# A fused attention and two-MLP kernel: q, k and v laid out by the host, and the scale moved into the step that takes the minimum

## The chip, the cores and the metric

The kernel runs on one core of one Trainium2 chip, as a single launch. The metric is the device time of an execution in microseconds; the work that the host does on the arrays before the launch is not in it.

## What is computed

The reference has three stages. The first is causal attention over a batch of 4, 8 heads, 576 tokens and a head size of 64, with a bias from a running sum:

```python
scores = scale * np.matmul(q, k.transpose(0, 1, 3, 2))
cum = np.cumsum(np.maximum(s, 0.0), axis=-1)
bias = -(cum[:, :, :, None] - cum[:, :, None, :])
scores = np.where(causal, -1000000000.0, scores + np.minimum(bias, 0.0))
...
attn = np.exp(scores)
attn = attn / (np.sum(attn, axis=-1, keepdims=True) + 1e-09)
return np.matmul(attn, v).astype(np.float32)
```

Its result is laid out as 2304 tokens by 512. The second stage is an MLP of 512 to 2048 to 512, `(s * relu(x @ w_in)**2 + b) @ w_out`. The third takes the elementwise maximum of three products, `max(x @ w1, x @ w2, x @ w3) @ w_out`, 512 to 768 to 512. Everything is float32.

## The kernel before, in words

**Stages.** The MLPs run as products of values split into two parts (`mm3`, lines 242 to 246: three matmuls for each product). The hidden units of the first MLP are halved: the first half ("a") is computed while attention still runs, the second half ("b") after it, and then comes the third stage. The weights are split into their two parts on the fly (`weight_steps`, lines 258 to 289): one load, an ACT step at line 273, and steps on DVE, ACT or POOL.

**Jobs.** Attention works on pairs of heads: 16 pairs, four for each batch. The four pairs of the first batch are done in two jobs each, "A" (queries 0 to 319) and "B" (the others); the twelve other pairs are one job "W" each. So there are 20 jobs. For each job the kernel loads q and k with tokens on the partitions (`load_tokens`, lines 427 to 434: one DMA for each head's full chunks of 128 tokens at line 432, and one for a remainder at line 434), turns chunks of both heads on TensorE (`turn`, line 476), and copies them out of PSUM on ACT or DVE (`copy_qk`, line 486, through `copy`, lines 233 to 237); the copy of q multiplies by minus the scale. v is loaded by the same `load_tokens` and is used as it lands. The tiles of q and k in turned form, and those of v, alternate between two buffers; the tiles as loaded, `qn` and `kn`, exist once.

**Scores.** A job has up to six units (a chunk of queries by a range of keys). `qk` (lines 488 to 497) writes the scores of both heads of a unit into two PSUM banks (line 493) and adds the bias through a one-hot matrix and the table `dd` (line 495). `least` (line 507, on DVE) adds the causal mask `late_keys`, multiplies by a scale operand that is 1.0, and writes the result and its row minimum. `expo` (line 513, ACT) takes the exponential, `turn_p` (line 554) turns the probabilities on TensorE, `copy_p` takes them out of PSUM, and `av` (line 573) multiplies by v. `x_copy` (line 578) divides by the row sums, and `x_lo` stores x (line 590).

**The start.** s is loaded four times into groups of 32 partitions on ACT's DMA queue (line 327). DVE clears the unused rows of `qn` and `kn` (line 333), clips s (line 339), takes the running sum (line 340) and the differences to the middle of each query chunk (line 345); ACT and DVE split them into `dd` (lines 348 and 349). Meanwhile TensorE runs `warm` (line 449): 26 transposes whose result nobody reads.

**The order.** All steps after the start are put into a list with costs, due times and needs, and a planner (`Plan.order`, lines 89 to 184) lays them out for each engine; each engine then executes its own list in order. Attention steps have due times from a nominal period for a job; MLP steps fill what is left. Three things in that list belong to the change: the needs of the loads (lines 669 to 676), the steps `turn` and `copy` with their share of the ring of four PSUM banks called `sm`, and the assumed lengths of the start on DVE and ACT (line 642). All loads and stores except those of s are issued by SP.

Of the kernel before, what the change touches and what calls it, by code (L numbers as in the profile page):

```python
# [8 lines left out]
F32 = mybir.dt.float32  # L9
# [5 lines left out]
ALU = mybir.AluOpType  # L15
# [3 lines left out]
P = 128  # L19
BIG = 1.0e9  # L20
# [6 lines left out]
WARM = 26  # L27
# [4 lines left out]
Q_LOAD = -15.0  # L32
K_LOAD = -14.0
V_LOAD = 2.0
# [158 lines left out]
def fused_kernel(ctx, tc, q, k, v, s, w_in, w_out, ms, mb, w1, w2, w3, w_fin, out,  # L193
                 f_split=8):
    nc = tc.nc
    B, H, S, D = q.shape
    NT, DM = out.shape
    DFF = w_in.shape[1]
    DF2 = w1.shape[1]
    NP = H // 2  # L200
# [3 lines left out]
    NC = (S + P - 1) // P  # L204
    LAST = S - (NC - 1) * P
# [120 lines left out]
    for g in range(4):  # L326
        nc.scalar.dma_start(s0[g * NH:(g + 1) * NH], s.rearrange("b h s -> (b h) s"))
    qn, kn = (atp.tile([P, NC, 2, D], F32, name=x) for x in ("qn", "kn"))
    vn = [atp.tile([P, NC, 2, D], F32, name=f"vn{i}") for i in range(2)]
    SHORT = (SPLIT // P, NC - 1)  # L330
    for t in (qn, kn):
        for c in SHORT:
            nc.vector.memset(t[LAST:, c], 0.0)
# [9 lines left out]
    def difference(i):  # L343
        mid = QS[i] + QN[i] // 2
        nc.vector.tensor_scalar(df[:, OFF[i]:OFF[i] + W[i]], cum[:, :W[i]], -1.0, cum[:, mid:mid + 1], op0=ALU.mult, op1=ALU.add)
# [20 lines left out]
    nc.gpsimd.affine_select(out=late_keys[:, ZK - P:], in_=late_keys[:, ZK - P:], pattern=[[-1, P]], compare_op=ALU.is_ge, fill=BIG, base=0, channel_multiplier=1)  # L366
# [60 lines left out]
    def load_tokens(dst, src, p, a, b):  # L427

        bt, hp = divmod(p, NP)
        full, rem = divmod(b - a, P)  # L430
        for j in range(2):
            nc.sync.dma_start(dst[:, :full, j, :], src[bt, 2 * hp + j, a:a + full * P, :].rearrange("(c p) d -> p c d", p=P))
        if rem:
            nc.sync.dma_start(dst[:rem, full, :, :], src[bt, 2 * hp:2 * hp + 2, b - rem:b, :].rearrange("h p d -> p h d"))

    def load_q(job):
        load_tokens(qn, q, job.p, job.q0, job.q1)

    def load_k(job):
        load_tokens(kn, k, job.p, 0, job.keys)  # L440

    def load_v(job):
        load_tokens(vn[job.n % 2], v, job.p, 0, job.keys)
# [26 lines left out]
    def turn(job, key, t, a, b):  # L470

        chunks = range((b - a + P - 1) // P)
        for c0 in range(0, len(chunks), 4):
            ps = bank("pr")
            for c in chunks[c0:c0 + 4]:
                nc.tensor.transpose(ps[:, (c - c0) * P:(c - c0 + 1) * P], t[:, c, :, :], ident)  # L476
            end = min(a + (c0 + 4) * P, b)
            pr[key, job.n, c0 // 4] = (ps, slice(a + c0 * P, end), slice(0, end - a - c0 * P))

    def copy_qk(job, key, z, on):  # L480

        to = {"q": qt, "k": kt}[key]
        if job.n not in to:
            to[job.n] = atp.tile([P, S], F32, name=key, tag=f"{key}{job.n % 2}")
        ps, at, fr = pr.pop((key, job.n, z))
        copy(to[job.n][:, at], ps[:, fr], on, -scale if key == "q" else None)

# [11 lines left out]
    def least(job, u, j):  # L499

        i, k0, k1 = UNITS[u][:3]
        n = QN[i]
        if u == job.units[0]:
            mns[job.n, j] = atp.tile([P, NC], F32, name="mn", tag=f"mn{j}{job.n % 2}")
        mn = mns[job.n, j][:n, i:i + 1]
        a = 0 if k1 < W[i] else ZK - max(k1 - k0, P)
        nc.vector.tensor_tensor_reduce(out=pp[j][i][:n, k0:k1], in0=late_keys[:n, a:a + k1 - k0], in1=ps_.pop((job.n, u, j))[:n, :k1 - k0], scale=1.0,  # L507
                                       scalar=mn if k0 else HUGE, op0=ALU.add, op1=ALU.min, accum_out=mn)
# [85 lines left out]
    def bank(name):  # L594
        ring, z = plan.slot(*BANK)
        return psum.tile([P, 512], F32, name=name, tag=f"b{BANK[ring] + z}")
# [45 lines left out]
    for e, cost in (("DVE", 9.75), ("ACT", 8.8), ("Pool", 5.0)):  # L642
        add(("pre", e), e, cost, -1e9, [], lambda: None)
# [8 lines left out]
    for job in jobs:  # L652
# [16 lines left out]
        for key, load, when, src, q0, q1 in (("q", load_q, Q_LOAD, qn, job.q0, job.q1), ("k", load_k, K_LOAD, kn, 0, job.keys)):  # L669
            add((key, n), "SP", (3, q1 - q0), t0 + when, [("turn", key, n - 1)], load, job, **a)  # L670
            z = range(((q1 - q0 + P - 1) // P + 3) // 4)
            add(("turn", key, n), "PE", 0.109 * ((q1 - q0 + P - 1) // P), tp, [(key, n)], turn, job, key, src, q0, q1, take=[("sm", [("copy", key, n, y)]) for y in z], **a)
            for y in z:
                m = min(4 * P, q1 - q0 - y * 4 * P)
                add(("copy", key, n, y), {"ACT": act_ps(m), "DVE": dve_ps(m)}, 0, tp + 0.1, [("turn", key, n)] + [("qk", n - 2, u) for u in range(6)], copy_qk, job, key, y, **a)
        add(("v", n), "SP", (3, job.keys), t0 + V_LOAD, [("av", n - 2, g) for g in (jobs[n - 2].groups if n > 1 else ())], load_v, job, **a)
        add(("oh", n), "Pool", 0.3, tp, [("qk", n - 2, u) for u in range(6)], one_hot, job, **a)

        for x, u in enumerate(units):
# [3 lines left out]
            ready = [("oh", n)] + [("copy", z, n, y) for z in "qk" for y in range(2)]  # L683
# [431 lines left out]

# [23 lines left out]
```

## Time and profile before

| what | before |
|---|---|
| median of 3 runs | 980.51 us (976.75 to 981.84) |
| the profiled execution | 975.74 us |
| its span, first to last instruction | 973.9 us |
| mean granted clock of TensorE | 0.993 of full speed |
| TensorE busy | 98% of the span |
| DVE, ACT, POOL busy | 51%, 47%, 17% |

Times are microseconds from the start of the span unless ns is said. PE is TensorE, PEld its weight loads, which overlap with matmuls; DVE, ACT and POOL are the vector, scalar and general engines; SPq and ACTq are instructions of the queues of SP and ACT, DMA issues among them. Ends of matmuls are modelled, so two neighbours overlap in a list in order of time, and it is the distance of their starts that tells how long each held the engine. "<-" behind an idle time names what ended it.

### The profile page before, as it was taken

To read this page: it belongs to the slowest core of one execution; us is meant where nothing else is said; L and a number is where in the kernel's file an instruction comes from. 1 tells how busy PE (TensorE), PEld (TensorE's weight loads), DVE (VectorE), ACT (ScalarE), POOL (GpSimd) and SP (SyncE) were. 2 spreads that over 40 slices of the span, in tenths; PEclk is the share of its full clock that TensorE was granted. 3 is DMA by queue.
4 is the path that set the end of the run, shared out by engine and by line. 5 is a ranking of instruction groups with operands and counts; after the bars stand their busy time and mean duration, and the time that the engine had idled before them with its cause. 6 is when DMAs were issued, how large, how long until landed. Compare 5 with 4: busy or idle time off the path is not lost.

```text
span 973.9 us, 17863 instructions
## 1 busy us (share of the span) xinstructions
PE 952.4 (98%) x6558; PEld 867.9 (89%) x6558; DVE 495.7 (51%) x1324; ACT 454.3 (47%) x1221; POOL 168.7 (17%) x270
## 2 busy tenths in 40 slices
PE   7899999999999999999999999999999999999997
PEld 5577788888789789999999999999999999999997
DVE  6898867778663432132778786426621222222221
ACT  5888678778774572232555454333321212121111
POOL 2333123212203022222333232220000000000000
PEclk7999999999999999999999999999999999999999
DMA  6655555565442101561444444225220201010000
GB/s 187 175 144 132 149 160 138 167 178 146 137 123 73 52 8 47 190 225 36 128 139 131 132 126 132 81 69 166 62 66 1 63 3 49 17 39 11 2 31 34
DMA packets 120632, 96.11 MB, mean 99 GB/s; under 512 B 70240, under 2 KB 104032, under 8 KB 120544
## 3 DMA queue, kind: packets, MB, share of 16 engines
q1 hardware_dynamic: 120352, 94.67, 32.8%
q8 instruction: 52, 0.85, 0.4%
q10 hardware_dynamic: 192, 0.30, 0.1%
q14 instruction: 36, 0.29, 0.1%
HBM read 67.67 MB, written 27.26 MB: 97 GB/s over the span
## 4 chain that ended last, share of the span: by engine, by line
PE 88%; DMA 4%; DVE 2%; ACT 2%; SPq 1%; issue 1%; POOL 1%; DVEq 0%; ACTq 0%; POOLq 0%
PE mm L244 23%; PE mm L246 22%; PE mm L245 22%; PE ps L493 6%; PE pt L554 6%; PE px L573 5%; PE pr L476 2%; PE ps L495 1%; PE pr L544 1%; DMA wb_in<-wb_d 1%; DMA xs<-x_d 1%; DMA wg<-in_moe_w_in_dram 1%; DMA stage<-in_moe_w_out_dram 0%; POOL ga L240 0%; DMA wst<-in_moe_w_out_dram 0%
## 5 line engine op out<-in xcount | busy, mean ns | idle before, releaser
L244 PE MATMUL mm<-yh,wt 128*128 128x384 f32 x432 | 146.2, 339 | 0.0
L246 PE MATMUL mm<-yh,wt 128*128 128x384 f32 x432 | 146.2, 338 | 0.0
L245 PE MATMUL mm<-yl,wt 128*128 128x384 f32 x432 | 146.2, 338 | 0.0
L1056 DVE TENSOR_TENSOR u<-mm,u 128x384 f32<-128x384 f32 x72 | 40.1, 558 | 190.2 <-PE mm L246 190.2
L909 ACT ACTIVATE g<-g 128x256 f32<-128x256 f32 (+1 forms) x128 | 56.3, 440 | 136.5 <-DVE g L905 135.8
L905 DVE TENSOR_SCALAR g<-mm 128x256 f32<-128x256 f32 (+1 forms) x128 | 58.1, 455 | 78.8 <-PE mm L246 68.1
L513 ACT ACTIVATE pp<-pp,mn 64x64 f32<-64x64 f32 (+4 forms) x160 | 88.4, 556 | 19.1 <-DVE mn L507 18.9
L244 PE MATMUL mm<-xhi,wa_in 128*128 128x320 f32 (+1 forms) x256 | 82.4, 322 | 0.0
L244 PEld LDWEIGHTS mm<-yh,wt 128*128 128x128 f32 x432 | 81.1, 188 | 1.3
L245 PEld LDWEIGHTS mm<-yl,wt 128*128 128x128 f32 x432 | 81.1, 188 | 1.3
L244 PE MATMUL mm<-ga,wa_out 128*128 128x320 f32 (+2 forms) x256 | 82.2, 321 | 0.0
L554 PE MATMUL pt<-ident,pp 128*128 128x128 f32 x480 | 78.0, 281 | 3.2 <-DVE mn L507 1.4
L233 ACT ACTIVATE pt<-pt 128x256 f32<-128x256 f32 (+3 forms) x186 | 74.0, 434 | 15.4 <-PE pt L554 12.1
L240 POOL TENSOR_TENSOR gbl<-g,gbh 128x320 fp32r<-128x320 f32 (+1 forms) x64 | 55.8, 874 | 145.9 <-ACT gbh L233 143.6
L246 PEld LDWEIGHTS mm<-yh,wt 128*128 128x128 f32 x432 | 81.1, 188 | 0.0
L1060 ACT ACTIVATE hh<-u 128x384 fp32r<-128x384 f32 x36 | 18.9, 525 | 133.1 <-DVE u L1056 133.1
L507 DVE CUSTOM_DVE_ANT_0 pp<-late_keys,ps 64x64 f32<-64x64 f32 (+4 forms) x160 | 62.2, 421 | 33.2 <-PE ps L495 32.7
L246 PE MATMUL mm<-ga,wa_out 128*128 128x320 f32 (+2 forms) x256 | 76.0, 297 | 1.8 <-DVE wa_out L288 1.8
L240 POOL TENSOR_TENSOR ga<-g,ga 128x320 fp32r<-128x320 f32 (+1 forms) x64 | 53.3, 833 | 135.3 <-ACT ga L233 119.9
L245 PE MATMUL mm<-xlo,wa_in 128*128 128x320 f32 (+1 forms) x256 | 75.8, 296 | 1.0 <-POOL xlo L240 1.0
L245 PE MATMUL mm<-ga,wa_out 128*128 128x320 f32 (+2 forms) x256 | 75.9, 296 | 0.8 <-POOL ga L240 0.8
L246 PE MATMUL mm<-xbh,wb_in 128*128 128x320 f32 (+1 forms) x256 | 75.8, 296 | 0.0
(172 smaller groups left out, 2364.0 us busy)
## 6 DMA issues: line engine op xcount, KB each, us to landing
wst<-in_moe_w_dram SPq DMA_DIRECT2D x24, 384.0 KB, 3.8
wb_d<-wbs SPq DMA_DIRECT2D x21, 256.0 KB, 2.8
out_dram<-o SPq DMA_DIRECT2D x18, 256.0 KB, 2.0
kn<-in_k_dram SPq DMA_DIRECT2D x32, 128.0 KB, 2.9
vn<-in_v_dram SPq DMA_DIRECT2D x32, 128.0 KB, 2.7
wst<-in_moe_w_out_dram SPq DMA_DIRECT2D x8, 512.0 KB, 4.1
wb_in<-wb_d SPq DMA_DIRECT2D x8, 512.0 KB, 7.2
wb_out<-wb_d SPq DMA_DIRECT2D x8, 512.0 KB, 10.0
```

Source lines behind the costliest of these rows:

```text
L233: nc.scalar.activation(dst, src, AF.Copy, scale=1.0 if scale is None else scale)
L240: ENGINES[on].tensor_tensor(dst, a, b, op=ALU.subtract)
L244: nc.tensor.matmul(ps, lhs[0], rhs[0], start=first, stop=False)
L245: nc.tensor.matmul(ps, lhs[0], rhs[1], start=False, stop=False)
L246: nc.tensor.matmul(ps, lhs[1], rhs[0], start=False, stop=last)
L493: nc.tensor.matmul(ps[:, :k1 - k0], qt[job.n][r, QS[i]:QS[i] + P], kt[job.n][r, k0:k1], start=True, stop=False)
L507: nc.vector.tensor_tensor_reduce(out=pp[j][i][:n, k0:k1], in0=late_keys[:n, a:a + k1 - k0], in1=ps_.pop((job.n, u, j))[:n, :k1 - k0], scal ...
L513: nc.scalar.activation(p[:n, :w], p[:n, :w], AF.Exp, bias=mns[job.n, j][:n, i:i + 1], scale=-1.0, accum_out=sums[job.n % 2][:n, j, i:i + 1])
L554: nc.tensor.transpose(pt[:, c - c0, :], pp[j][i][:, c * P:(c + 1) * P], ident)
L573: nc.tensor.matmul(px_[job.n][hf][j * D:(j + 1) * D, a0 - h0:h1 - h0], vn[job.n % 2][:, c, j, :], columns(job, pr["p", job.n, j], c, c + 1 ...
L905: nc.vector.tensor_scalar(st["g", f], st["u", f][:, :n], 0.0, None, op0=ALU.max)
L909: nc.scalar.activation(st["g", f], st["g", f], AF.Square)
```

## The change

The host lays out q and k as [pair, 2 x 64, tokens] and v as [pair, tokens, 2 x 64]; `kernel()` passes each input through `_lay_out` before the launch. q and k are loaded straight into the two alternating tiles that the score matmuls read, by one DMA each (`load_qk`), and v by one DMA for the full chunks and one for a remainder (`load_v`). `turn` and `copy_qk` are gone, with the tiles `qn` and `kn` and their clearing. A load of q or k now waits for the score matmuls of the job before the last, which read the same tile; before, it waited for the transposes of the last job. The scale goes into `least` as minus the scale; the mask and the bias differences are divided by it beforehand. Two of the four loads of s go to SP's queue. `warm` has 40 transposes instead of 26, and the lengths that the planner assumes for the start are shorter.

```diff
@@ -24,7 +24,7 @@
 ST2 = 3
 COLD = 8
 D_AT = -2.0
-WARM = 26
+WARM = 40
 
 PACE_3 = 2
 
@@ -193,8 +193,9 @@
 def fused_kernel(ctx, tc, q, k, v, s, w_in, w_out, ms, mb, w1, w2, w3, w_fin, out,
                  f_split=8):
     nc = tc.nc
-    B, H, S, D = q.shape
+    B, H, S = s.shape
     NT, DM = out.shape
+    D = DM // H
     DFF = w_in.shape[1]
     DF2 = w1.shape[1]
     NP = H // 2
@@ -324,13 +325,9 @@
     s4 = atp.tile([P, 4, S], F32, name="s4", tag="p3")
     s0, cum, ones, dh = (s4[:, i, :] for i in range(4))
     for g in range(4):
-        nc.scalar.dma_start(s0[g * NH:(g + 1) * NH], s.rearrange("b h s -> (b h) s"))
-    qn, kn = (atp.tile([P, NC, 2, D], F32, name=x) for x in ("qn", "kn"))
+        (nc.sync if g < 2 else nc.scalar).dma_start(s0[g * NH:(g + 1) * NH], s.rearrange("b h s -> (b h) s"))
     vn = [atp.tile([P, NC, 2, D], F32, name=f"vn{i}") for i in range(2)]
     SHORT = (SPLIT // P, NC - 1)
-    for t in (qn, kn):
-        for c in SHORT:
-            nc.vector.memset(t[LAST:, c], 0.0)
     nc.vector.memset(ones, 1.0)
     lower = const.tile([P, 1], F32, name="lower")
     nc.vector.memset(lower, 0.0)
@@ -342,7 +339,7 @@
     df = atp.tile([P, OFF[-1] + W[-1]], F32, name="df", tag="p2")
     def difference(i):
         mid = QS[i] + QN[i] // 2
-        nc.vector.tensor_scalar(df[:, OFF[i]:OFF[i] + W[i]], cum[:, :W[i]], -1.0, cum[:, mid:mid + 1], op0=ALU.mult, op1=ALU.add)
+        nc.vector.tensor_scalar(df[:, OFF[i]:OFF[i] + W[i]], cum[:, :W[i]], cum[:, mid:mid + 1], 1.0 / scale, op0=ALU.subtract, op1=ALU.mult)
 
     def split_d(a, b):
         nc.scalar.activation(dh[:, :b - a].bitcast(F32R), df[:, a:b], AF.Copy)
@@ -363,7 +360,7 @@
     ZK = W[NC - 2]
     late_keys = atp.tile([P, ZK], F32, name="late_keys")
     nc.gpsimd.memset(late_keys, 0.0)
-    nc.gpsimd.affine_select(out=late_keys[:, ZK - P:], in_=late_keys[:, ZK - P:], pattern=[[-1, P]], compare_op=ALU.is_ge, fill=BIG, base=0, channel_multiplier=1)
+    nc.gpsimd.affine_select(out=late_keys[:, ZK - P:], in_=late_keys[:, ZK - P:], pattern=[[-1, P]], compare_op=ALU.is_ge, fill=-BIG / scale, base=0, channel_multiplier=1)
 
     for t in vn:
         for c in SHORT:
@@ -424,23 +421,19 @@
         nc.sync.dma_start(s_sb, ms.partition_broadcast(P))
         nc.sync.dma_start(b_sb, mb.partition_broadcast(P))
 
-    def load_tokens(dst, src, p, a, b):
-
-        bt, hp = divmod(p, NP)
-        full, rem = divmod(b - a, P)
-        for j in range(2):
-            nc.sync.dma_start(dst[:, :full, j, :], src[bt, 2 * hp + j, a:a + full * P, :].rearrange("(c p) d -> p c d", p=P))
+    def load_qk(job, key):
+
+        to, src, a, b = (qt, q, job.q0, job.q1) if key == "q" else (kt, k, 0, job.keys)
+        to[job.n] = atp.tile([P, S], F32, name=key, tag=f"{key}{job.n % 2}")
+        nc.sync.dma_start(to[job.n][:, a:b], src[job.p, :, a:b])
+
+    def load_v(job):
+
+        full, rem = divmod(job.keys, P)
+        t = vn[job.n % 2].rearrange("p c h d -> p c (h d)")
+        nc.sync.dma_start(t[:, :full], v[job.p, :full * P].rearrange("(c p) d -> p c d", p=P))
         if rem:
-            nc.sync.dma_start(dst[:rem, full, :, :], src[bt, 2 * hp:2 * hp + 2, b - rem:b, :].rearrange("h p d -> p h d"))
-
-    def load_q(job):
-        load_tokens(qn, q, job.p, job.q0, job.q1)
-
-    def load_k(job):
-        load_tokens(kn, k, job.p, 0, job.keys)
-
-    def load_v(job):
-        load_tokens(vn[job.n % 2], v, job.p, 0, job.keys)
+            nc.sync.dma_start(t[:rem, full], v[job.p, full * P:job.keys])
 
     def warm():
 
@@ -466,24 +459,6 @@
 
 
     UNITS = [(i, 0, QS[i] + QN[i], 0, i + 1) for i in range(NC - 1)] + [(NC - 1, 0, S // 2, 0, 3), (NC - 1, S // 2, S, 3, NC)]
-
-    def turn(job, key, t, a, b):
-
-        chunks = range((b - a + P - 1) // P)
-        for c0 in range(0, len(chunks), 4):
-            ps = bank("pr")
-            for c in chunks[c0:c0 + 4]:
-                nc.tensor.transpose(ps[:, (c - c0) * P:(c - c0 + 1) * P], t[:, c, :, :], ident)
-            end = min(a + (c0 + 4) * P, b)
-            pr[key, job.n, c0 // 4] = (ps, slice(a + c0 * P, end), slice(0, end - a - c0 * P))
-
-    def copy_qk(job, key, z, on):
-
-        to = {"q": qt, "k": kt}[key]
-        if job.n not in to:
-            to[job.n] = atp.tile([P, S], F32, name=key, tag=f"{key}{job.n % 2}")
-        ps, at, fr = pr.pop((key, job.n, z))
-        copy(to[job.n][:, at], ps[:, fr], on, -scale if key == "q" else None)
 
     def qk(job, u):
 
@@ -504,7 +479,7 @@
             mns[job.n, j] = atp.tile([P, NC], F32, name="mn", tag=f"mn{j}{job.n % 2}")
         mn = mns[job.n, j][:n, i:i + 1]
         a = 0 if k1 < W[i] else ZK - max(k1 - k0, P)
-        nc.vector.tensor_tensor_reduce(out=pp[j][i][:n, k0:k1], in0=late_keys[:n, a:a + k1 - k0], in1=ps_.pop((job.n, u, j))[:n, :k1 - k0], scale=1.0,
+        nc.vector.tensor_tensor_reduce(out=pp[j][i][:n, k0:k1], in0=late_keys[:n, a:a + k1 - k0], in1=ps_.pop((job.n, u, j))[:n, :k1 - k0], scale=-scale,
                                        scalar=mn if k0 else HUGE, op0=ALU.add, op1=ALU.min, accum_out=mn)
 
     def expo(job, i, j):
@@ -639,7 +614,7 @@
 
     add(("begin",), {"SP": 1.05}, 0, -1e9, [], lambda: None)
     add(("s_b",), "SP", (2, 2), 30.0, [], load_sb)
-    for e, cost in (("DVE", 9.75), ("ACT", 8.8), ("Pool", 5.0)):
+    for e, cost in (("DVE", 7.7), ("ACT", 6.8), ("Pool", 5.0)):
         add(("pre", e), e, cost, -1e9, [], lambda: None)
     add(("warm",), "PE", 0.213 * WARM / 2, -1e9, [], warm, take=[("sm", [("warm",)])])
     for i in range(3, NC):
@@ -666,21 +641,16 @@
 
 
         tp = t0 + TURN
-        for key, load, when, src, q0, q1 in (("q", load_q, Q_LOAD, qn, job.q0, job.q1), ("k", load_k, K_LOAD, kn, 0, job.keys)):
-            add((key, n), "SP", (3, q1 - q0), t0 + when, [("turn", key, n - 1)], load, job, **a)
-            z = range(((q1 - q0 + P - 1) // P + 3) // 4)
-            add(("turn", key, n), "PE", 0.109 * ((q1 - q0 + P - 1) // P), tp, [(key, n)], turn, job, key, src, q0, q1, take=[("sm", [("copy", key, n, y)]) for y in z], **a)
-            for y in z:
-                m = min(4 * P, q1 - q0 - y * 4 * P)
-                add(("copy", key, n, y), {"ACT": act_ps(m), "DVE": dve_ps(m)}, 0, tp + 0.1, [("turn", key, n)] + [("qk", n - 2, u) for u in range(6)], copy_qk, job, key, y, **a)
-        add(("v", n), "SP", (3, job.keys), t0 + V_LOAD, [("av", n - 2, g) for g in (jobs[n - 2].groups if n > 1 else ())], load_v, job, **a)
+        for key, when, m in (("q", Q_LOAD, job.q1 - job.q0), ("k", K_LOAD, job.keys)):
+            add((key, n), "SP", (1, m), t0 + when, [("qk", n - 2, u) for u in range(6)], load_qk, job, key, **a)
+        add(("v", n), "SP", (2, job.keys), t0 + V_LOAD, [("av", n - 2, g) for g in (jobs[n - 2].groups if n > 1 else ())], load_v, job, **a)
         add(("oh", n), "Pool", 0.3, tp, [("qk", n - 2, u) for u in range(6)], one_hot, job, **a)
 
         for x, u in enumerate(units):
             i, k0, k1, c0, c1 = UNITS[u]
             same = [("turn_p", n - 1, z, j) for z in range(6) if UNITS[z][0] == i for j in range(2)]
             order = [("after", ("qk", n, units[x - 1]))] if x else [("after", ("qk", n - 1, jobs[n - 1].units[-1]))] if n else []
-            ready = [("oh", n)] + [("copy", z, n, y) for z in "qk" for y in range(2)]
+            ready = [("oh", n), ("q", n), ("k", n)]
             add(("qk", n, u), "PE", 5 * (k1 - k0) / 2400 + 0.25, at[u], ready + [("dd", i) if i > 2 else ("pre", "DVE")] + [("after", z) for z in same] + order, qk, job, u,
                 take=[("sm", [("least", n, u, j)]) for j in range(2)], **a)
             for j in range(2):
@@ -1113,6 +1083,16 @@
 _OUTS = [((2304, 512), 'float32')]
 
 
+def _lay_out(name, a):
+
+    import numpy as _np
+    if name in ("q", "k", "v"):
+        b, h, n, d = a.shape
+        a = a.reshape(b, h // 2, 2, n, d).transpose((0, 1, 2, 4, 3) if name != "v" else (0, 1, 3, 2, 4))
+        a = a.reshape(b * h // 2, *((2 * d, n) if name != "v" else (n, 2 * d)))
+    return _np.ascontiguousarray(a)
+
+
 def kernel(**inputs):
     import numpy as _np
     import concourse.bacc as _bacc
```

## Rows read from the trace of the kernel before

**Rows 1.** the page, part 1: busy time, share of the span, instructions

```profile
PE 952.4 (98%) x6558; PEld 867.9 (89%) x6558; DVE 495.7 (51%) x1324; ACT 454.3 (47%) x1221; POOL 168.7 (17%) x270
```

**Rows 2.** busy time by stretch: stretch, length, engines (instructions), PEclk, DMA share, GB/s

```profile
0.00:60.00 60.00, 49.17 (x312) 35.99 (x313) 45.98 (x143) 43.53 (x131) 15.69 (x48) 0.91 0.66 175
60.00:120.00 60.00, 58.00 (x432) 45.64 (x430) 54.75 (x148) 46.78 (x128) 17.78 (x26) 1.00 0.51 137
120.00:280.00 160.00, 158.56 (x1274) 127.13 (x1272) 117.57 (x424) 129.07 (x409) 34.94 (x64) 1.00 0.54 154
```

**Rows 3.** TensorE in order of time, 152.31 to 153.21: start, length, what

```profile
152.31 0.28 PE L246 MATMUL mm<-xhi,wa_in 128*128 128x256 f32 x1
152.42 0.71 PE L476 MATMUL pr<-ident,qn 128*128 128x128 f32 x5
152.89 0.36 PE L244 MATMUL mm<-xhi,wa_in 128*128 128x256 f32 x1
153.09 0.28 PE L245 MATMUL mm<-xlo,wa_in 128*128 128x256 f32 x1
```

**Rows 4.** the order of time, first 13 us: start, length, what [idle before]

```profile
0.73 2.96 ACTq L327 DMA_DIRECT2D s<-in_s_dram  x4
...
1.74 4.66 PE L449 MATMUL warm<-ident 128*128 128x128 f32 x26 [1.74 <-POOL ident masks.py:199]
...
5.46 0.47 DVE L339 TENSOR_SCALAR s<-s 128x576 f32<-128x576 f32 x1 [3.00 <-DMA s<-in_s_dram]
...
6.82 0.59 SPq L269 DMA_DIRECT2D wg<-in_moe_w_in_dram  x1
...
8.89 0.82 DVE L349 SCALAR_TENSOR_TENSOR dd<-s,lower,df 128x576 fp32r<-128x576 f32 x1
9.08 0.43 ACT L233 ACTIVATE k<-pr 128x320 f32<-128x320 f32 x1
...
9.56 0.44 PE L493 MATMUL ps<-k,q 64*128 64x64 f32 x4 [2.51 <-ACT k L233]
...
12.21 0.66 ACT L273 ACTIVATE wg<-wg 128x512 f32<-128x512 f32 x1 [2.15 <-DMA wg<-in_moe_w_in_dram]
```

**Rows 5.** busy time by stretch, the start, columns as in Rows 2

```profile
2.00:5.00 3.00, 3.00 (x16) 3.00 (x16) 0.39 (x6) 1.28 (x1) 2.61 (x17) 1.00 0.74 182
5.00:6.00 1.00, 1.00 (x10) 1.00 (x10) 0.51 (x2) 0.00 (x1) 1.00 (x2) 1.00 0.43 74
...
12.00:22.00 10.00, 8.92 (x36) 6.48 (x36) 7.43 (x23) 7.71 (x25) 0.29 (x1) 0.50 0.62 175
```

**Rows 6.** line 476 (transposes of q and k) alone, TensorE and weight loads

```profile
0.00:60.00 60.00, 8.44 (x42) 5.59 (x42) 0.91 0.66 175
60.00:120.00 60.00, 4.31 (x30) 3.50 (x30) 1.00 0.51 137
120.00:340.00 220.00, 14.39 (x100) 11.26 (x100) 1.00 0.46 131
```

**Rows 7.** lines 432 and 434, issues: ns min/median/max; landing for line 432

```profile
L432 SPq DMA_DIRECT2D qn<-in_q_dram x40: 368/468/892, 0.7 to 314.1; - x40
...
L434 SPq DMA_DIRECT2D kn<-in_k_dram x20: 601/642/875, 3.9 to 316.6; - x20
...
DMA to landing us min/median/max: 1.9/2.8/5.0
```

**Rows 8.** the chain of waits, 120 to 150 us: starts of a job's av

```profile
124.27 2.42 PE px L573 x24
...
143.99 2.42 PE px L573 x24
```

**Rows 9.** DVE groups by shape, first 20 us: busy us, mean ns, idle before

```profile
L345 DVE TENSOR_SCALAR df<-s 128x576 f32<-128x576 f32 x1 | 0.5, 516 | 0.0
L339 DVE TENSOR_SCALAR s<-s 128x576 f32<-128x576 f32 x1 | 0.5, 471 | 3.0 <-DMA s<-in_s_dram 3.0
```

**Rows 10.** waits of SP's queue: us in total, times, longest

```profile
SPq L590 <- DVE x L578: 55.9, 4, 29.4
```

More of the change, by code (lines that the diff above doesn't have):

```diff
@@ L1125 @@
     for name in _INS:
-        a = _np.ascontiguousarray(inputs[name])
+        a = _lay_out(name, inputs[name])
         if a.dtype == _np.float64:
```

## The prediction

> **What bounds the kernel now.** I read the page's engine totals first: TensorE is busy for 98% of the span [rows 1]. Such a share is an average, so next I cut the attention part into stretches [rows 2]. From 60 to 280 us TensorE is busy 58.00 of 60 and 158.56 of 160 us, at the full clock; DVE is nearly as full from 60 to 120 us (54.75 of 60) and has room afterwards (117.57 of 160). Before 60 us no engine is full: TensorE 49.17, DVE 45.98, ACT 43.53 of 60. Since the ends of matmuls are modelled, I checked the order in time [rows 3]: MLP matmuls and attention steps start right behind each other, no row shows idle time ahead of it, and after five transposes the next matmul starts 0.47 us later. So from 60 us on TensorE carries the time: the MLP products of one batch fill what the attention of the next leaves open, and work taken from it is worth its own length.
>
> The first 12 us are another regime [rows 4]. DVE gets s at 5.46 us, after ACT needed 2.96 us to issue four loads; the bias table is written from 8.89, for 0.82 us, and the first scores start at 9.56. ACT then stands in its own queue from about 10.06 until a weight load lands at 12.2; SP had issued that load only at 6.82, behind ten other issues. SP's issues, that load and ACT make one string of waits. TensorE, with little to do meanwhile, falls to half clock (1.2 of 2.4 GHz) for 12 to 22 us [rows 5].
>
> **The change, part by part.**
>
> *Transposes of q and k.* All 172 go: 42 before 60 us, 30 from 60 to 120, 100 later [rows 6]. One costs 0.11 us: 0.47 for the five of [rows 3], and the matmul behind them holds the engine 0.20 us where the one ahead of them held it 0.11, 0.56 in all. After 120 us: 100 x 0.11 = 11.0 us, which I count whole. From 60 to 120: 30 x 0.11 = 3.3, but DVE may end that stretch (weight conversion, 91% busy); I count half, 1.6, between 0 and 3.3. Before 60: 42 x 0.11 = 4.6, weighted with TensorE's busy share 49.17/60: 3.8; bounds 0 (latency governs all of it) and the 8.44 us that the profile books for these instructions [rows 6], some at half clock.
>
> *Their copies.* ACT or DVE loses 68 copies (four for each W job, two for each A, three for each B), 0.43 us for a 320-wide one [rows 4], and the PSUM banks they held. After 60 us this lies beside TensorE's work: nothing. Before it, it is what lets the 3.8 above be real; not counted twice.
>
> *Loads.* q, k and v take 176 issues on SP now (line 432: 40 for each of the three; line 434: 20 each for k and v, 16 for q). They become 20 + 20 + 40 = 80; at 0.47 to 0.64 us each [rows 7] SP saves some 50 us, nearly all of it beside other work. What counts is the start: ahead of the second weight load stand two s loads, q, k, a weight load and two v issues, seven where there were ten. Those ten took 6.82 - 0.74 = 6.1 us, so the load goes out 3 x 0.61 = 1.8 us sooner, and ACT's stand at 12.21 ends 1.8 us sooner. Meanwhile s arrives after two issues on ACT instead of four, 2.96 / 2 = 1.5 us sooner, so the first scores come at about 8.1 to 8.3. q and k, now third and fourth on SP, land by some 5.7 (four issues, then 2.8 to landing [rows 7]): covered by 2.4 us. I take 1.8 for the start, bounds 0 and 2.2 (the whole of ACT's stand).
>
> *A later release.* A q or k load now goes straight into the tile that the matmuls of job n-2 read, so SP waits for the last of these where it waited for a transpose of job n-1. One job of the steady part lasts 19.7 us (124.27 to 143.99 [rows 8]); issue and landing need 0.5 + 2.8. Cost: nothing, under a cover of 16 us. Queued behind the waiting issue on SP are weight loads, v and stores of x and y0; the second rival prices its loss.
>
> *Fourteen more warm-up transposes.* At the pace of 5 to 6 us, 10 in 1 us [rows 5], they add 1.5 us to a run that ends at 1.74 + 4.66 = 6.4 [rows 4]: 7.9, before the scores can start. Cost nothing, lower bound 0. At the pace of 2 to 5 us (16 in 3 us) they would take 2.6 and delay the scores by up to 0.9. I take 0, as the later pace is the nearer row. The doubling at 5 us came after nothing but warm-up transposes. The Trainium skill (TensorE: Matmul & The Clock Gate, Part 4: PE-mode transpose) says that transposes do not bring the full clock because they do not count as busy; by it the warm-up would stay at the slow pace and the sum would be 0.9 us worse. The row speaks against it.
>
> *Half clock.* 12 to 22 us run at half clock with TensorE busy 8.92 of 10, ACT 7.71 and DVE 7.43 [rows 5]. With scores and ACT sooner the fall may be avoided or come in a shorter stretch. At full clock ACT would bound the stretch, so at most 10 - 7.71 = 2.3 us is to be had. Bounds 0 and 2.3; I take 1.5, as the gap ahead of it is what the load and s changes shorten.
>
> *Scale.* It moves into an operand of the minimum step, 192 instructions (16 pairs, 6 units, 2 heads); no row shows that step with another scale. Nearest: a tensor-scalar with one operation takes 471 ns, with two 516 [rows 9]. Between 0 and 192 x 0.045 = 8.6 us of DVE, mostly in stretches where DVE has room: 0. The bias differences stay one two-operation instruction: 0. The dropped memsets lie in DVE's wait for s: 0.
>
> **Sum.** 1.8 + 3.8 + 1.5 + 1.6 + 11.0 = 19.7 us. The profiled execution took 975.74 us (span 973.9), so 956.0 on its terms; the median of the runs is 980.51, 4.8 above it, and the prediction is on that: 980.51 - 19.7 = 960.8. After attention nothing changes: the MLP stages come as early as TensorE gets to them.
>
> **Rivals.**
> 1. DVE or latency governs everything up to 120 us; only the 100 later transposes count: 980.51 - 11.0 = 969.5. For it: DVE's 91%. Against: the first scores come sooner, which gives DVE its work sooner. Chance 0.11.
> 2. Slower: the direct load is exposed. SP issues in order; if a store of x stands ahead of the q load (one such wait lasted 29.4 us [rows 10]), the load goes out after the 16 us of cover and TensorE stops for up to 3.3 us per job. It decides from 6 of 20 jobs on (19.7 / 3.3); if the twelve late jobs pay it all, +39.6 - 19.7 gives 1000.4. Against: MLP products lie between the jobs, so TensorE need not stop at once. Chance 0.03.
> 3. TensorE had slack from 60 to 280 us, and what goes was hidden in it. Weight loads are busy only 45.64 and 127.13 us there [rows 2]. Then only the first stretch gains, 1.8 + 3.8 + 1.5 = 7.1: 973.4. Against: [rows 3] show no gap, and a weight load that is shorter than the matmul it feeds leaves its share under one without idle time. The Trainium skill (Trainium Kernel Development and Optimization, Performance Expectations) calls the busy time of matmuls a bad metric and that of weight loads a good one; this is its reading. Chance 0.06.
> 4. The early part opens up wholly: start 2.2, half clock 2.3, transposes 8.4 and all later ones 14.3, 27.2 us: 953.3. Chance 0.10, since no engine is full there.
> The forecast keeps 0.70.
>
> **Numbers.** The ends of the range are rival 1 (969.5, so 970) and rival 4 less the 3.8 us by which the fastest shown run lies below the median: 949.5, so 950. Beyond them lie rivals 2 and 3 and stray tails, under 0.2. Half a per cent, 4.9 us, is about what a measurement tells from no change. Forecast, rivals 1 and 4 and most of 3 are faster by more: 0.94. Same: 0.03, from the small half of rival 3. Slower: 0.03.
>
> **What would show it.** No row of line 476 and no copies out of pr to q or k; 80 issues for q, k and v; s at DVE near 4.0 us, first scores near 8.2, ACT's wait for the weight load gone; a shorter half-clock stretch; a steady job 1.1 us shorter than 19.7; the MLP part from 440 us on simply shifted. It is wrong if TensorE shows waits for q or k loads, if jobs keep their length with idle time in TensorE, or if the minimum step gets longer and DVE ends the waits.

## The result and the profile after

| what | before | after |
|---|---|---|
| median | 978.66 us (4 runs, 976.75 to 981.84) | 953.62 us (4 runs, 951.73 to 955.46) |
| ratio, 95% interval | | 0.974 (0.970 to 0.978) |
| profiled execution | 975.74 us | 951.73 us |
| its span | 973.9 us | 949.9 us |

The kernel became 25.0 us faster by the medians and 24.0 by the profiled executions. The forecast was 960.8, with a range of 950 to 970. Of the 7.2 us between it and the median, 5.3 are a gain that was sized too small (19.7), and 1.9 come from the kernel before, whose median was 980.51 when the forecast was made and is 978.66 with the fourth run.

The page of the kernel after, part 1 (busy time, share of the span, instructions), beside [rows 1]:

```profile
PE 929.6 (98%) x6400; PEld 853.3 (90%) x6400; DVE 490.7 (52%) x1318; ACT 431.4 (45%) x1154; POOL 166.7 (18%) x271
```

TensorE's busy time fell by 22.8 us (952.4 to 929.6), and its idle time by 1.2 (973.9 - 952.4 = 21.5, 949.9 - 929.6 = 20.3): the gain is work that went, with hardly any wait dissolved. ACT lost 22.9 us of work, DVE 5.0. Ends of matmuls are modelled, so I also added up in both traces how long each instruction held TensorE, from its start to the next start, idle time left out. The 172 transposes held it for 21.0 us before (7.3 before 60 us, 3.4 from 60 to 120, 10.4 later). Against that, the longer warm-up took 2.5 us more, the MLP matmuls 3.4 less, the other attention steps 0.7 less, and idle time between them fell by 1.0: together about the 24.0 of the two spans. In the two later traces of the changed kernel each of these terms is the same within 1.0 us.

Busy time by stretch after the change, columns as in [rows 2]:

```profile
0.00:60.00 60.00, 53.23 (x355) 40.42 (x356) 50.52 (x159) 46.64 (x140) 19.46 (x54) 0.91 0.58 181
60.00:120.00 60.00, 53.75 (x397) 41.88 (x395) 52.64 (x150) 43.38 (x122) 12.31 (x22) 0.97 0.49 152
120.00:280.00 160.00, 159.88 (x1278) 132.39 (x1275) 118.89 (x435) 119.52 (x378) 37.85 (x69) 1.00 0.52 159
```

The first 60 us hold 4.1 us more TensorE work than before (53.23 against 49.17), although the transposes are gone from them; 2.4 of it is the longer warm-up. Counted without warm-up and transposes, TensorE has done 315 instructions by 60 us (355 - 40) where it had done 244 (312 - 26 - 42). The next 60 us hold 4.3 less work (53.75 against 58.00): a new wait. By 120 us it is ahead by 66 instructions instead of 71 (712 against 646). From 120 us on TensorE is full as before. The waits of TensorE from 60 to 120 us after the change (total, times, longest) name it:

```profile
PE mm L247 <- DVE wa_out L289: 3.5, 2, 2.7
PE mm L245 <- ACT wa_out L234: 1.8, 1, 1.8
```

Before, the same wait for the second weights of the first half was 1.8 us in all:

```profile
PE mm L246 <- DVE wa_out L288: 1.8, 2, 1.1
```

Attention now runs ahead, the MLP products reach these weights sooner, and DVE and ACT have not finished them. The waits cost more than their length: behind them the granted clock falls, which it did not before (1.00 in this stretch).

```profile
100.00:120.00 20.00, 17.51 (x129) 13.32 (x129) 14.78 (x52) 12.96 (x43) 2.34 (x5) 0.91 0.40 127
```

With the two levels of 2.4 and 1.2 GHz, a mean of 0.91 over 20 us is 3.6 us at the lower one; by this estimate 1.8 us of TensorE's work are lost.

The start, in order of time after the change (beside [rows 4]):

```profile
0.73 0.89 ACTq L328 DMA_DIRECT2D s<-in_s_dram  x2
...
0.73 0.87 SPq L328 DMA_DIRECT2D s<-in_s_dram  x2
...
1.74 7.04 PE L442 MATMUL warm<-ident 128*128 128x128 f32 x40 [1.74 <-POOL ident masks.py:199]
...
3.85 0.52 DVE L336 TENSOR_SCALAR s<-s 128x576 f32<-128x576 f32 x1 [2.11 <-DMA s<-in_s_dram]
...
5.10 0.57 SPq L270 DMA_DIRECT2D wg<-in_moe_w_in_dram  x1
...
7.85 0.82 DVE L346 SCALAR_TENSOR_TENSOR dd<-s,lower,df 128x576 fp32r<-128x576 f32 x1 [0.75 <-ACT s L345]
...
8.71 0.44 PE L468 MATMUL ps<-k,q 64*128 64x64 f32 x4
...
9.45 0.66 ACT L274 ACTIVATE wg<-wg 128x512 f32<-128x512 f32 x1 [1.63 <-DMA wg<-in_moe_w_in_dram]
...
10.14 0.43 DVE L277 TENSOR_SCALAR wg<-wg 128x512 int32<-128x512 int32 x1 [1.47 <-ACT wg L274]
...
11.28 0.67 ACT L274 ACTIVATE wg<-wg 128x512 f32<-128x512 f32 x1 [1.18 <-DMA wg<-in_moe_w_in_dram]
...
12.14 0.80 PE L468 MATMUL ps<-k,q 64*128 64x320 f32 x3 [2.42 <-DVE mn L482]
```

s reaches DVE 1.6 us sooner, the first scores come 0.85 sooner, and the second weight load is issued 1.7 sooner. ACT still stands for weight loads, now twice, 1.63 and 1.18 us, and through DVE's step behind the first of them TensorE stands 2.42 us before the third unit. The warm-up ends at 1.74 + 7.04 = 8.78, not at 7.9, and the bias table at 7.85 + 0.82 = 8.67. So the first scores, at 8.71, start right behind the warm-up, and the matmul that adds the bias starts at 8.95, 0.28 behind the table.

The stretch from 12 to 22 us after the change, beside [rows 5], and the one behind it:

```profile
12.00:22.00 10.00, 8.75 (x40) 5.72 (x42) 8.49 (x35) 9.32 (x35) 0.98 (x4) 0.58 0.67 236
22.00:32.00 10.00, 9.00 (x70) 6.48 (x69) 8.23 (x26) 8.38 (x31) 1.56 (x3) 0.91 0.47 136
```

The clock falls as before (0.58 of full speed on average, where it was 0.50), after TensorE stood 2.42 us; before the change it had stood 2.51 us ahead of the first scores and 2.05 us more at 12.69.

### The profile page after: what moved, and what is told of

Its sections match the earlier page's. It is cut to its first block, busy times and chain, and to the rows that moved or that the text cites. A ratio compares the mean times of both kernels' runs of the same rounds, so it can differ in the third digit from the quotient of the medians.

```text
span 949.9 us, 17281 instructions
## 1 busy us (share of the span) xinstructions
PE 929.6 (98%) x6400; PEld 853.3 (90%) x6400; DVE 490.7 (52%) x1318; ACT 431.4 (45%) x1154; POOL 166.7 (18%) x271
## 4 chain that ended last, share of the span: by engine, by line
PE 89%; DMA 4%; ACT 2%; DVE 2%; SPq 1%; issue 1%; POOL 1%; DVEq 0%; ACTq 0%; POOLq 0%
PE mm L245 24%; PE mm L246 23%; PE mm L247 23%; PE ps L468 6%; PE pt L529 6%; PE px L548 5%; PE ps L470 1%; PE pr L519 1%; DMA xs<-x_d 1%; DMA wb_in<-wb_d 1%; DMA wg<-in_moe_w_in_dram 1%; ACT pp L488 1%; POOL ga L241 0%; DMA wst<-in_moe_w_out_dram 0%; DMA wbs<-in_moe_w_in_dram 0%
## 5 line engine op out<-in xcount | busy, mean ns | idle before, releaser
L234 ACT ACTIVATE pt<-pt 128x256 f32<-128x256 f32 (+3 forms) x182 | 72.0, 436 | 21.5 <-PE pt L529 17.9
L245 PE MATMUL mm<-xhi,wa_in 128*128 128x320 f32 (+1 forms) x256 | 79.9, 312 | 0.0
L1030 ACT ACTIVATE hh<-u 128x384 fp32r<-128x384 f32 x36 | 18.9, 525 | 133.9 <-DVE u L1026 133.9
L247 PE MATMUL mm<-xbh,wb_in 128*128 128x320 f32 (+1 forms) x256 | 75.8, 296 | 0.0
L246 PE MATMUL mm<-xbl,wb_in 128*128 128x320 f32 (+1 forms) x256 | 75.8, 296 | 0.0
L245 PE MATMUL mm<-xbh,wb_in 128*128 128x320 f32 (+1 forms) x256 | 75.8, 296 | 0.0
```

What stands on the lines that cost most here:

```text
L234: nc.scalar.activation(dst, src, AF.Copy, scale=1.0 if scale is None else scale)
L245: nc.tensor.matmul(ps, lhs[0], rhs[0], start=first, stop=False)
L246: nc.tensor.matmul(ps, lhs[0], rhs[1], start=False, stop=False)
L247: nc.tensor.matmul(ps, lhs[1], rhs[0], start=False, stop=last)
```

## The experiments

The changed kernel was timed three times in all, with medians of 953.62, 953.14 and 954.14 us; where a run has no changed kernel beside it, 953.6 is the measure. This holds for the planned copies, transposes and both, and for the filled gap; the kernel before took 976.60 us beside these four, and 977.69 and 978.24 beside the others, so their distances from 953.6 may be 1 to 2 us too small.

**The changed kernel as the measure.**

> The changed kernel as it is, as the measure for the others on this chip. Both theories: ratio to the kernel before 0.974, between 0.970 and 0.978.

953.14 us, ratio 0.975 (0.972 to 0.978).

**Transposes put back, unknown to the planner.** Edit, in `qk` ahead of the first scores:

```diff
+        if u == job.units[0]:
+            for _ in range((job.q1 - job.q0 + P - 1) // P + (job.keys + P - 1) // P):
+                nc.tensor.transpose(both[0][1][:, :P], kt[job.n][:, :P], ident)
```

> The changed kernel with 172 transposes of the loaded keys put back on TensorE alone, ahead of the first scores of each job, into a bank that the scores then overwrite; no copies, no loads, no new order, and a planner that knows nothing of them. They are extra work and change no value. Theory (TensorE's own work governs): 172 x 0.11 = 18.9 us slower than the changed kernel, 16 to 21, so 6 us at most below the kernel before. Rival 1 (the gain came from copies, PSUM banks and issues on SP, and TensorE had slack): under 6 us slower.

970.32 us, ratio 0.9925 (0.990 to 0.995): 17.2 us slower than the changed kernel, 0.10 us for each of the 172. No copy, no DMA and no bank came back with them, so TensorE's own time is worth nearly its length. That is within the 16 to 21 expected. Rival 1 of this run, that TensorE had slack (rival 3 of the prediction), falls.

**Copies put back, unknown to the planner.** In the same place:

```diff
+        if u == job.units[0]:
+            for m in (job.q1 - job.q0, job.keys):
+                for n in [min(512, m)] + [m - 512] * (m > 512):
+                    nc.scalar.activation(spare[:, :n], kt[job.n][:, :n], AF.Copy)
```

> The changed kernel with 68 copies put back on ACT alone, from the loaded keys into a tile that nobody reads, in the widths of the copies of q and k before; no value changes. ACT gets some 28 us of work back. Theory (TensorE's work governs): under 3 us slower than the changed kernel, all of it before 60 us. Rival 1 (ACT, not TensorE, was relieved): 8 us or more slower.

971.15 us, 0.993 (0.991 to 0.996): 18.0 us slower: the theory (under 3) missed, and the number lies in the rival's range. Together with the run above it would explain 35 us of a gain of 25, so the two prices do not add. The waits of TensorE in this run show what happened:

```profile
PE pt L534 <- ACT pp L493: 13.5, 15, 1.1
PE mm L247 <- DVE wa_out L289: 3.5, 2, 2.7
```

15 times TensorE waits for an exponential, 13.5 us in all; the changed kernel has at most 0.4 us of this wait. The order of every engine was laid out for an ACT without these copies. An exponential that comes late by the length of a copy stops TensorE at the transposes of the probabilities, whatever MLP work stands behind them. This suggests that the order, which doesn't know the step, sets the price, and not ACT's work (30.2 us in this run). To tell the two apart, both edits were made again as planned steps.

**Copies as planned steps.** Edit (the reload of the tile also needs them):

```diff
+        for key, m in (("q", job.q1 - job.q0), ("k", job.keys)):
+            for y, w in enumerate([min(512, m)] + [m - 512] * (m > 512)):
+                add(("dup", key, n, y), {"ACT": act_ps(w), "DVE": dve_ps(w)}, 0, tp + 0.1, [("k", n)], dup, job, w, **a)
```

> The changed kernel with the 68 copies put back as steps of the planner, on ACT or DVE, from the loaded keys into tiles that nobody reads; the planner knows their costs and lays the other steps out around them. The run with unplanned copies was 18 us slower than the changed kernel, with TensorE waiting for the exponentials. Theory now (TensorE's own work governs, and unplanned copies only broke an order made without them): under 4 us slower than the changed kernel. Rival 1 (ACT's relief carries the gain): 12 to 19 us slower.

958.38 us, 0.9825 (0.980 to 0.9845): 4.8 us above 953.6, a little more than expected, and far from rival 1. It is not the same load, though: the planner put 41 copies on ACT (18.2 us) and 27 on DVE (9.3 us), where the kernel before had 64 on ACT and 4 on DVE. So it prices the copies as a planner places them; the full load on ACT, planned, comes only in the run with both steps. By stretch:

```profile
0.00:60.00 60.00, 50.20 (x318) 37.14 (x320) 45.62 (x144) 46.96 (x142) 17.73 (x50) 0.86 0.54 168
60.00:120.00 60.00, 54.14 (x384) 43.00 (x381) 56.31 (x160) 44.84 (x122) 19.27 (x26) 0.97 0.48 149
120.00:280.00 160.00, 159.21 (x1269) 128.78 (x1268) 123.70 (x456) 129.42 (x413) 35.70 (x65) 1.00 0.51 162
```

TensorE loses 3.0 us in the first 60 (50.20 against 53.23), and does 318 instructions there where the changed kernel does 355; afterwards it is nearly as full. ACT gets 9.9 us more work from 120 to 280 us, and TensorE is only 0.7 us less busy there.

**Transposes as planned steps.** The same with `add(("turn", key, n), "PE", 0.109 * chunks, ...)`, each group holding a bank of the ring only while it runs.

> The changed kernel with the 172 transposes put back on TensorE as steps of the planner, each group in a PSUM bank that it holds only while it runs; no copies, loads as changed. Theory: 14 to 19 us slower than the changed kernel. Rival (the planner hides them in TensorE's waits when it knows of them): under 8 us.

975.22 us, 0.999 (0.998 to 1.000): 21.6 us above 953.6, and above the 14 to 19 expected. With TensorE's transposes alone the time is 0.1% (1.4 us) below the kernel before, and its interval reaches 1.000: the gain is gone. Knowing of them, the planner hid none. Why the planned ones came out 4.4 us above the unplanned ones (21.6 - 17.2) is only partly known: in the profiled executions they hold TensorE for 24.5 us, from start to start, where the unplanned ones hold it for 21.7, and TensorE is idle for 18.5 us against 14.3. What in the order makes these differences stays open.

**Both as planned steps**, transposes into banks that are held until the copy, as before the change; only the scores no longer wait for them:

```diff
+            add(("turn", key, n), "PE", 0.109 * ((m + P - 1) // P), tp, [("k", n)], turn, job, key, m, take=[("sm", [("dup", key, n, y)]) for y in z], **a)
+            for y in z:
+                w = min(512, m - 512 * y)
+                add(("dup", key, n, y), {"ACT": act_ps(w), "DVE": dve_ps(w)}, 0, tp + 0.1, [("turn", key, n)], dup, job, key, y, w, **a)
```

> The changed kernel with transposes and their copies put back together as steps of the planner, with the PSUM banks held from a transpose to its copy; the scores don't wait for them, and loads, scale and start are as changed. Theory: 16 to 22 us slower than the changed kernel; what is then left to the kernel before (2 to 8 us) belongs to loads, start and the wait of scores for their own transposes. Rival 1: clearly more than the sum of the two runs with one of them each.

973.99 us, 0.9975 (0.996 to 0.999): 20.4 us above 953.6, within what was expected, and no more than the transposes alone. Here 65 copies are on ACT, 26.5 us, about as before the change: beside the transposes, the copies on ACT add nothing. What is left to the kernel before is 0.13 to 0.37%, 1.3 to 3.6 us: loads, start, and the wait of the scores for their own transposes.

**The scale alone**, in the kernel before:

```diff
-        copy(to[job.n][:, at], ps[:, fr], on, -scale if key == "q" else None)
+        copy(to[job.n][:, at], ps[:, fr], on)
...
-... scale=1.0,
+... scale=-scale,
```

with mask and differences as in the change.

> The kernel before with only the scale moved: the copy of q no longer multiplies, the minimum step multiplies by minus the scale, mask and differences are divided by it. Theory: same as the kernel before within 0.3%, and the minimum step keeps its lengths (615 ns for 448 columns, 482 for 320). Rival: each such step gets up to 45 ns longer and the time rises by up to 3 us, where DVE ends the waits before 110 us.

977.67 us, ratio 1.000 (0.998 to 1.003). The groups of the minimum step in this run (busy us, mean ns):

```profile
L507 DVE CUSTOM_DVE_ANT_0 pp<-late_keys,ps 128x448 f32<-128x448 f32 x32 | 18.6, 615 | 8.3 <-PE ps L495 8.3
...
L507 DVE CUSTOM_DVE_ANT_0 pp<-late_keys,ps 128x320 f32<-128x320 f32 x32 | 14.4, 481 | 10.0 <-PE ps L495 9.8
```

In the kernel before, with scale 1.0:

```profile
L507 DVE CUSTOM_DVE_ANT_0 pp<-late_keys,ps 128x448 f32<-128x448 f32 x32 | 18.6, 615 | 7.7 <-PE ps L495 7.7
...
L507 DVE CUSTOM_DVE_ANT_0 pp<-late_keys,ps 128x320 f32<-128x320 f32 x32 | 14.4, 482 | 8.7 <-PE ps L495 8.6
```

The lengths are the same: the scale costs nothing.

**The gap filled.** 20 transposes of the identity behind the second unit of the first job:

```diff
+        if job.n == 0 and u == 1:
+            idle = psum.tile([P, 512], F32, name="idle", tag="b7")
+            for _ in range(20):
+                nc.tensor.transpose(idle[:, :P], ident, ident)
```

> The changed kernel with 20 more transposes of the identity matrix behind the second unit of the first job, where TensorE stands from 9.7 to 12.1 us, into a bank that nobody uses then; extra work, no value changes. It asks what the half clock after that gap costs. Theory (ACT and DVE bound the early stretch): the fall to half clock comes later or not at all, and the time falls by 0 to 2.3 us. Rival: the full 4.5 us that half clock takes from TensorE's work in 10 us comes back.

954.93 us, 0.9775 (0.975 to 0.980): no gain, where 0 to 2.3 us were expected. The filler in order of time, and the stretches beside the two rows of the changed kernel above:

```profile
9.50 2.40 PE L476 MATMUL idle<-ident 128*128 128x128 f32 x20
...
12.00:22.00 10.00, 7.76 (x40) 4.96 (x42) 8.03 (x32) 9.60 (x34) 1.25 (x4) 0.74 0.70 244
22.00:32.00 10.00, 9.04 (x71) 6.62 (x71) 8.48 (x26) 8.59 (x32) 1.56 (x3) 0.92 0.48 135
```

From 12 to 22 us the clock is granted 0.74 on average where it was 0.58; TensorE is busy a microsecond less, and does the same 40 matmuls. ACT is busy 9.60 of 10. Without warm-up and filler, TensorE does 44, 132 and 143 instructions in the first three stretches of 20 us, exactly as many as in the changed kernel. So the part of the half clock that the filler took away cost nothing: it slowed an engine that waits anyway. That the rest of it (0.74 is not 1.00) costs nothing either was not tried.

**26 warm-up transposes**, in the changed kernel and its order (`for _ in range(26)`). For comparison the changed kernel ran again beside it.

> The changed kernel as it is, beside the three others of this call. Ratio to the kernel before 0.975, between 0.972 and 0.978.

> The changed kernel with 26 warm-up transposes instead of 40, in the same order. Theory (nothing waits for the warm-up, and half clock in the first 30 us costs nothing, as the run with the filled gap showed): same as the changed kernel within 2 us. Rival: the clock falls sooner or for longer and the time rises by 2.3 to 4.5 us.

954.14 and 955.06 us: 0.9 apart, and the intervals (0.976, 0.9735 to 0.9785; 0.977, 0.975 to 0.979) overlap nearly whole. The additional 14 cannot be told from nothing. With 26 the first scores start at 6.46, but the matmul that adds the bias waits for the table and starts at 8.79, where it starts at 8.95 with 40.

**All of s on ACT's queue**, in the changed kernel:

```diff
-        (nc.sync if g < 2 else nc.scalar).dma_start(s0[g * NH:(g + 1) * NH], ...)
+        nc.scalar.dma_start(s0[g * NH:(g + 1) * NH], ...)
```

> The changed kernel with all four loads of s on ACT's queue again, two issues fewer at the head of SP's. Theory: s reaches DVE some 1 to 1.5 us later, the first scores come that much later, and the time rises by 0 to 1.5 us. Rival: the weight load goes out 0.9 us sooner on SP, and the time falls by up to 1 us.

956.29 us, 0.978 (0.976 to 0.980): 2.2 us above the run beside it, with intervals that overlap (0.976, 0.9735 to 0.9785), so the size is uncertain. Its start in order of time:

```profile
0.73 3.32 ACTq L328 DMA_DIRECT2D s<-in_s_dram  x4
...
8.50 0.46 DVE L336 TENSOR_SCALAR s<-s 128x576 f32<-128x576 f32 x1 [6.77 <-DMA s<-in_s_dram]
...
11.92 0.82 DVE L346 SCALAR_TENSOR_TENSOR dd<-s,lower,df 128x576 fp32r<-128x576 f32 x1
```

s lands at 8.5 us, 4.7 later than in the changed kernel and 3.0 later than in the kernel before, and the bias table follows. That is at least three times the delay of 1 to 1.5 us that was expected. Some 4 us at the start become about 2 at the end.

**Weights sooner**, after the new wait of the changed kernel:

```diff
-PER = {"A": 5.6, "B": 8.0, "W": 15.0}
+PER = {"A": 6.9, "B": 8.8, "W": 16.3}
-W_1 = -0.633
-W_S1 = 4.607
-W_2 = 29.041
-W_S2 = 2.532
+W_1 = -0.09
+W_S1 = 4.43
+W_2 = 23.54
+W_S2 = 2.55
...
-                    [("w", "a", x, 8) for x in WX] + [("av", ...)
+                    [("w", "a", x, 8) for x in range(16)] + [("av", ...)
```

> A version after what the profile of the changed kernel shows: TensorE waits there some 6 us for the second weights of the first half (wa_out) between 80 and 110 us. The weights of the second half are not begun before all of those are done, and due times of weights and jobs are shifted. Theory: these waits shrink by 2 to 5 us and the time by as much. Rival: the DVE work only moves, and TensorE waits elsewhere for as long; within 1 us of the changed kernel.

949.11 us, 0.9706 (0.969 to 0.973): 5.0 us below the changed kernel beside it (954.14), at the upper end of what was expected. Its stretches show where:

```profile
0.00:60.00 60.00, 51.14 (x333) 36.93 (x334) 50.78 (x152) 43.82 (x131) 16.52 (x51) 0.91 0.57 176
60.00:120.00 60.00, 59.53 (x441) 46.90 (x441) 52.52 (x162) 46.48 (x131) 14.61 (x23) 1.00 0.51 159
```

From 60 to 120 us TensorE is busy 59.53 us instead of 53.75, the wait for `wa_out` is no longer among its waits, and the granted clock stays at 1.00 there; 2.1 us of that are paid in the first 60. The edit shifts the jobs and the second half's weights together, so the 5.0 us belong to the new order as a whole and not to the one wait alone.

## Why the prediction held, step by step

**The total.** The mechanism was right, but that the sum came within 7.2 us is partly luck, since errors cancelled. The transposes brought more than was taken (21.0 us by their starts, against 16.4), the MLP matmuls some 3 us, of which the terms held only what stood right behind a transpose, and the terms for start and half clock (1.8 + 1.5) little: all idle time of TensorE together fell by about 1 us. Rival 4, everything early opens up, came nearer in number (953.3). Its full count of the transposes came true, the rest of its mechanism did not: the clock fell again, ACT stood for weight loads again, and from 60 to 120 us TensorE got less done than before.

**What bounds.** TensorE's own work from 60 us on, as read from [rows 2, 3]: put back alone, 172 transposes cost 17.2 and, planned, 21.6 us of the 25.0. The slack that the busy share of weight loads seems to leave (rival 3) is not there.

**Transposes.** This is the term that was mis-sized: 3.8 + 1.6 + 11.0 = 16.4 us was taken, with the early ones weighted down and those from 60 to 120 us halved. At 0.11 us each the full count is 18.9; by their starts they held TensorE for 21.0, 7.3 of it before 60 us, where some ran at half clock; putting them back cost 17.2 to 21.6. Where TensorE did not carry the time all along, the removed work still paid: the first 60 us took 315 instructions of the other work where they had taken 244. That TensorE, ACT and the banks hold that stretch in turn is my reading.

**Copies.** Costed at nothing beside the transposes, and that held: with the transposes put back too they add nothing. Put back alone and planned, partly on DVE, they cost 4.8 us, which the text did not say; the whole load on ACT alone, planned, was not tried.

**DVE from 60 to 120 us (rival 1).** Its mechanism came true, its total did not. The wait for weights that DVE and ACT had not finished grew from 1.8 to 5.3 us, the clock fell behind it, and the run with the weights sooner got 5.0 us back. So this stretch lost, where the prediction counted a gain of 1.6. But rival 1 let the stretch ahead of it gain nothing, and it gained.

**Start.** 1.8 us was taken from SP's issues. The load did go out 1.7 us sooner, but ACT and DVE stood for the next weight load instead; the first scores came 0.85 us sooner, held by the longer warm-up and then by the bias table. The loads of s, taken as 1.5 us of ACT's issue time, may matter more than that once the other loads go out early: 2.2 us by the medians of the run with all of s on ACT, though the intervals overlap. What the new start and the new loads gain over the old ones together is within the 1.3 to 3.6 us that the run with both steps put back leaves.

**Half clock.** 1.5 us was taken: wrong. The clock fell all the same, and a shorter fall gave nothing. The reading that ACT bounds the stretch was right, but the 2.3 us left beside it were not to be had: ACT was busy 9.32 of the 10 us after the change, not 7.71.

**Warm-up and scale.** Both at nothing, both right in the time. But the warm-up ran at the slow pace for longer than before, 6 transposes from 5 to 6 us where there were 10, and ended at 8.78 instead of 7.9; the table it had to be ahead of came at 8.67.

```profile
2.00:5.00 3.00, 3.00 (x16) 3.00 (x16) 1.12 (x2) 0.94 (x1) 2.60 (x15) 1.00 0.97 276
5.00:6.00 1.00, 1.00 (x6) 1.00 (x6) 0.96 (x3) 0.00 (x0) 1.00 (x3) 1.00 0.75 175
```

The starts of the transposes lie 0.21 us apart until 6.7 us and 0.11 from 6.9 on; so as in [rows 5] the pace doubled after nothing but transposes. The Trainium skill (TensorE: Matmul & The Clock Gate, Part 4: PE-mode transpose) says of transposes, measured there in bf16, that they do not bring the full clock; the pace in this trace speaks against it a second time. The granted clock reads 1.00 at either pace and doesn't show the change.

**The later release.** The wait moved to where it was expected, and no work of TensorE waits for q or k. The waits of SP's queue after the change:

```profile
SPq L428 <- PE ps L470: 23.1, 15, 3.1
```

23.1 us of SP standing still, with no row of TensorE waiting for a load of q or k: rival 2 did not come about.

**The check on the jobs.** A steady job was to be 1.1 us shorter than the 19.7 of [rows 8]. No such steady distance exists after the change. The same starts in the chain of waits:

```profile
114.84 2.43 PE px L548 x24
...
148.62 2.42 PE px L548 x24
...
163.59 2.43 PE px L548 x24
...
214.64 2.42 PE px L548 x24
...
250.68 2.40 PE px L548 x28
...
346.69 2.87 PE px L548 x32
```

15.0 us lie between 148.62 and 163.59, and 36.0 between 214.64 and 250.68: the jobs bunch, and the MLP products come in larger stretches between later ones. On average the check holds. The last of the twelve late jobs of the kernel before stands in its chain as

```profile
370.44 2.87 PE px L573 x32
```

so its eleven distances from 124.27 on have a mean of 22.4 us, and those after the change, from 114.84 to 346.69, one of 21.1. That the relief of ACT and of the banks lets them bunch is my reading and was not tried. It changes no sum, since the same work fills TensorE either way.

## What to carry to other kernels

Where one engine has its starts back to back and other work always fits in behind, price removed work at the time from its starts to the next and don't discount it by neighbours' loads; discount only what a neighbour must finish for the work that moves up, and look for that wait next (here the weights). Two steps that go together must be put back separately and together, and known to whatever lays out the order: a step that a fixed order doesn't know can show that order's slack and not the step's price. Look also at which engine the planner gives a step that was put back.

## What the runs showed that was not expected

Unplanned copies, 30.2 us on ACT, cost 18.0 us; planned ones, 18.2 us on ACT and 9.3 on DVE, cost 4.8.

The loads of s took until 8.5 us to land when all four went out on ACT's queue, the last issue ending at 4.05; in the kernel before, with the last issue ending at 3.69, s was there at 5.46. Earlier and larger loads on SP's queue went out meanwhile. That these took the DMA engines' time is my reading; it was not tried by itself.

A matmul of the MLP right behind a transpose or another attention step holds TensorE some 0.08 us longer than behind another MLP matmul (0.20 against 0.11 to 0.12 in [rows 3]; in both traces 0.20 against 0.12 as the median for 256 columns behind transposes of the probabilities, and 0.23 against 0.15 for 320). After the change there are fewer such places. The group of line 244 on `xhi`, line 245 after the change, in the pages before and after:

```profile
L244 PE MATMUL mm<-xhi,wa_in 128*128 128x320 f32 (+1 forms) x256 | 82.4, 322 | 0.0
...
L245 PE MATMUL mm<-xhi,wa_in 128*128 128x320 f32 (+1 forms) x256 | 79.9, 312 | 0.0
```

In the traces a matmul of this group stands right behind an attention step 75 times before and 48 times after. 27 x 0.08 = 2.2 us, most of the difference of 2.5. The other runs agree: with the unplanned transposes, which stand among attention steps, it is 48 times and 80.0 us, with both steps planned 74 times and 82.2 us.
